# Attention and mixer on one core: two more pairs turned by DMA instead of TensorE, and a turn of u moved from segment 7 to slot 6

## The chip, the cores and the metric

The kernel runs on one core of a Trainium2 chip. The metric is the device time of one execution in microseconds. In the profile's names PE is TensorE (its matmuls), PEld its weight loads, DVE VectorE, ACT ScalarE, POOL GpSimd and SP SyncE, whose queue starts most transfers. The landing of a transfer is the time from its issue to the moment its data are reported as there. A run counts as fast when it is at most 1.5% above the fastest of its kernel.

## The reference

Eight batches of cosine attention with 12 heads, 448 rows and 64 columns per head, followed by a mixer: over the rows ("tok"), then over the columns ("ch").

```python
q_n = q / (norm(q) + 1e-6);  k_n = k / (norm(k) + 1e-6)
x = softmax(q_n @ k_n.T / tau) @ v            # heads side by side: 8 x 448 x 768
u = x + (relu(x.T @ w_tok1) @ w_tok2).T
out = u + relu(u @ w_ch1) @ w_ch2
```

## The kernel before: the parts that matter

Heads go in pairs, six to a batch, 48 in all. Segment i of the main loop computes the scores of pair i, the weighted sum of pair i-1, and pieces ("units") of the last two matmuls of an earlier batch. Two turns (transposes) matter. q and k of a pair must be turned before the scores:

```python
def tpose(i, a0=0, a1=2):                       # TensorE, then DVE copies out of PSUM
    pst = ps.tile([128, a1 - a0, NCH, n], FP16, name=f"pst_{i}_{a0}", tag="b")
    ... eight nc.tensor.transpose ...
    nc.vector.tensor_copy(out=st["qk"][:, a0:a1], in_=pst[:])

def tpose_dma(i):                               # one DMA from SP's queue
    nc.sync.dma_start_transpose(out=st["qk"]..., in_=st["kq16"][:]...)
```

Pairs below `DMA_T0 = 16` use the first, the others the second. And u of each pair must be turned before the "ch" matmuls; for most pairs by DMA, for pairs 2 to 5 on TensorE:

```python
def upose_two(p0, p1):
    psT = ps.tile([128, 2, 4, 128], FP16, name=f"psT_{p0}_{p1}", tag="b")
    ... eight transposes of pairs p0 and p1 ...
    nc.scalar.activation(out=ut[0][:, p0:p1 + 1:p1 - p0], in_=psT[:], func=AF.Copy)
```

The loop (cut):

```python
for i in range(NPAIR + 1, NP_ALL):              # segments 7 to 47
    for c in range(KC): score(i, c)             # psS, wide tiles "s"
    if i == NPAIR + 1:                          # segment 7
        upose(i - 4, 2); tok2(i - 2, pe=True); pv_wide(i - 1)
        upose_two(2, 5); x_wide(i - 1); sums(i + 2)
    else:
        pv_rest(i - 1); pv(i - 1, 0); pv(i - 1, 1)          # psO, small tiles "b"
    ...
    side(i)              # POOL: squares(i+3), scaled(i+2); loads; tpose_dma(i+2)
    unit(True)           # psG or psF
    ...                  # last scores: psS or psQ
    if i > NPAIR + 1: tok2(i - 2)               # psU, then DVE adds x: u
    if i + 1 < DMA_T0: tpose(i + 1)             # pst
    if due(): unit(True)
    tok1(i - 1)                                 # psR, then DVE's max: rt
    sums(i + 3)
```

PSUM has two small tiles ("b": psO, psU, pst, psR) and three wide ones ("s": scores, psG, psF). "Slot 6" is the pass for pair 6, written out ahead of this loop.

## Time and profile before

| | before |
|---|---|
| time, median of the first three runs | 386.81 us (386.41 to 387.72) |
| span of the profiled run | 385.1 us |
| PE (matmul) busy | 97% |
| granted clock | 0.997 |

### The profile page before, as it was taken

To read this page: it belongs to the slowest core of one execution; us is meant where nothing else is said; L and a number is where in the kernel's file an instruction comes from. 1 tells how busy PE (TensorE), PEld (TensorE's weight loads), DVE (VectorE), ACT (ScalarE), POOL (GpSimd) and SP (SyncE) were. 2 spreads that over 40 slices of the span, in tenths; PEclk is the share of its full clock that TensorE was granted. 3 is DMA by queue.
4 is the path that set the end of the run, shared out by engine and by line. 5 is a ranking of instruction groups with operands and counts; after the bars stand their busy time and mean duration, and the time that the engine had idled before them with its cause. 6 is when DMAs were issued, how large, how long until landed. Compare 5 with 4: busy or idle time off the path is not lost.

```text
span 385.1 us, 10228 instructions
## 1 busy us (share of the span) xinstructions
PE 372.8 (97%) x4128; PEld 244.4 (63%) x4128; DVE 217.0 (56%) x517; ACT 227.8 (59%) x399; POOL 238.3 (62%) x383
## 2 busy tenths in 40 slices
PE   5989999999999999999999999999999999999995
PEld 5566666667657666667656666667666666665563
DVE  6789766777536674557545674656544673241041
ACT  5899787746665457855675456854675466601400
POOL 8799997978567577678567667768657733000000
PEclk9999999999999999999999999999999999999998
DMA  8999999993985878868894788968994755013022
GB/s 204 257 239 222 264 243 188 209 215 65 223 191 126 214 184 203 181 156 176 219 190 118 185 192 201 190 173 178 197 217 117 139 124 124 15 56 95 0 77 89
DMA packets 114879, 64.08 MB, mean 166 GB/s; under 512 B 71184, under 2 KB 111248, under 8 KB 114832
## 3 DMA queue, kind: packets, MB, share of 16 engines
q1 hardware_dynamic: 108400, 57.49, 65.8%
q0 software_dynamic: 5616, 5.21, 8.6%
q10 hardware_dynamic: 816, 0.73, 0.7%
q8 instruction: 32, 0.52, 0.6%
q14 instruction: 15, 0.12, 0.1%
HBM read 43.45 MB, written 11.01 MB: 141 GB/s over the span
## 4 chain that ended last, share of the span: by engine, by line
PE 89%; DMA 3%; ACT 2%; DVE 2%; POOL 2%; issue 0%; ACTq 0%; DVEq 0%; POOLq 0%
PE psF L463 28%; PE psG L447 28%; PE psO L362 9%; PE psS L323 8%; PE psU L412 5%; PE psR L398 5%; DMA w2n<-in_moe_w_tok_dram 2%; PE psQ L330 2%; ACT pt L324 1%; PE psO L345 1%; DMA qf<-in_q_dram 1%; DVE ssq L253 1%; POOL kq L276 1%; PE pst L300 1%; PE psO L380 1%; POOL sq L237 1%
## 5 line engine op out<-in xcount | busy, mean ns | idle before, releaser
L324 ACT ACTIVATE pt<-psS 128x896 f16<-128x896 f32 (+1 forms) x156 | 132.6, 916 | 57.7 <-PE psS L323 57.7
L447 PE MATMUL psG<-ut,wc1t 128*128 128x448 f16 x576 | 116.8, 352 | 0.4 <-ACT ut L437 0.4
L463 PE MATMUL psF<-wc2t,gt 128*128 128x384 f16 (+2 forms) x684 | 116.2, 323 | 0.0
L276 POOL TENSOR_TENSOR kq<-kf,rn 128x384 f16<-128x384 f32 (+1 forms) x48 | 42.9, 894 | 73.8 <-DVE rn L262 70.5
L463 PEld LDWEIGHTS <-gt 128*128 128x128 f16 x684 | 64.3, 98 | 38.0
L450 ACT ACTIVATE gt<-psG 128x448 f16<-128x448 f32 x96 | 51.9, 541 | 61.4 <-PE psG L447 61.3
L447 PEld LDWEIGHTS <-wc1t 128*128 128x128 f16 x576 | 53.9, 98 | 44.7 <-issue 0.6
L467 DVE TENSOR_TENSOR ost<-psF,u 128x384 f32<-128x384 f32 (+2 forms) x65 | 34.5, 531 | 57.1 <-PE psF L463 56.9
L253 DVE TENSOR_REDUCE ssq<-sq 128x15 f32<-128x960 f32 (+2 forms) x49 | 55.8, 1141 | 4.7 <-ACT sq L235 3.9
L401 DVE TENSOR_SCALAR rt<-psR 128x256 f16<-128x256 f32 x48 | 20.1, 419 | 59.3 <-PE psR L398 59.2
L276 POOL TENSOR_TENSOR kq<-qf,rn 112x512 f16<-112x512 f32 x45 | 47.0, 1045 | 3.0
L323 PE MATMUL psS<-qk 64*128 64x448 f16 x312 | 41.6, 359 | 2.7 <-DVE qk L302 2.3
L237 POOL TENSOR_TENSOR sq<-qf 112x512 f32<-112x512 f32 x39 | 40.6, 1040 | 0.0
L237 POOL TENSOR_TENSOR sq<-kf 128x384 f32<-128x384 f32 (+1 forms) x46 | 40.2, 873 | 0.0
L362 PE MATMUL psO<-vt,pt 128*128 128x65 f16 (+1 forms) x1024 | 39.1, 193 | 0.0
L362 PEld LDWEIGHTS <-pt 128*128 128x128 f16 (+1 forms) x1024 | 34.2, 97 | 3.6 <-PE psS L323 1.0
L366 DVE TENSOR_TENSOR x<-psO,rec 128x256 f16<-128x256 f32 x82 | 34.8, 425 | 2.8
L415 DVE TENSOR_TENSOR u<-psU,x 128x512 f16<-128x512 f32 x48 | 32.3, 674 | 3.9 <-PE psU L412 2.7
L398 PEld LDWEIGHTS <-w1t 128*128 128x128 f16 x384 | 25.1, 98 | 9.3 <-issue 2.4
L398 PE MATMUL psR<-x,w1t 128*128 128x128 f16 x384 | 29.3, 219 | 0.7 <-DVE u L415 0.7
L412 PEld LDWEIGHTS <-w2t 128*128 128x128 f16 x384 | 24.8, 98 | 7.3 <-issue 1.0
L412 PE MATMUL psU<-rt,w2t 128*128 128x128 f16 x384 | 29.3, 219 | 0.0
(57 smaller groups left out, 289.2 us busy)
## 6 DMA issues: line engine op xcount, KB each, us to landing
qf<-in_q_dram SPq DMA_DIRECT2D x48, 224.0 KB, 4.2
kf<-in_k_dram SPq DMA_DIRECT2D x36, 192.0 KB, 3.6
vf<-in_v_dram SPq DMA_DIRECT2D x36, 192.0 KB, 3.8
vf<-in_v_dram SPq DMA_DIRECT2D x12, 224.0 KB, 7.7
out_dram<-ost SPq DMA_DIRECT2D x8, 336.0 KB, 3.6
wc1t<-in_moe_w_ch_dram POOLq DMA_DIRECT2D x4, 576.0 KB, 9.6
wc2t<-in_moe_w_ch_dram POOLq DMA_DIRECT2D x2, 1152.0 KB, 12.8
out_dram<-ost SPq DMA_DIRECT2D x8, 288.0 KB, 3.6
```

The lines of the kernel that those rows point to most:

```text
L237: nc.gpsimd.tensor_mul(out=dst, in0=src, in1=src)
L253: nc.vector.tensor_reduce(out=st["ssq"][0:n, sl], in_=st["sq"][0:n, sl], axis=AXX.X, op=ALU.add)
L276: eng.tensor_tensor(out=kq[0:p, a, 0:n].rearrange("p c g e -> p g c e"), in0=st["kq"[a]][:].rearrange("p (g c) e -> p g c e", g=2), in1=_b ...
L323: nc.tensor.matmul(psS[:, hh, 0:S], qk[hb, c * n:c * n + 128], qm[hb], start=True, stop=True)
L324: nc.scalar.activation(out=pts[i % 2][0:n, 2 * S * c:2 * S * (c + 1)].rearrange("p (h s) -> p h s", h=2), in_=psS[0:n, :, 0:S], func=AF.Ex ...
L362: nc.tensor.matmul(psO[:, m, 0:E + 1], pts[i % 2][0:n, at:at + 128], vt[0:n, i % HP, nch * hh + c, 0:E + 1], start=(old(i) and c == 0), st ...
L366: nc.vector.tensor_tensor(out=st["x"][:, :, hh * E:(hh + 1) * E], in0=psO[:, :, 0:E], in1=_bcast_free(rec[:], E), op=ALU.mult)
L398: nc.tensor.matmul(psR[:, tt], w1t[:, w1[m], tt * 128:(tt + 1) * 128], st["x"][:, m], start=(m == 0), stop=(m == 3))
L412: nc.tensor.matmul(psU[:, m], w2t[:, tt, lo:lo + 128], st["rt"][:, tt], start=(tt == 0), stop=(tt == TT - 1))
L447: nc.tensor.matmul(psG[:, 0:S], wc1t[:, dt, ct * 128:(ct + 1) * 128], ut[b][:, dt].rearrange("p m s -> p (m s)")[:, lo:lo + S], start=(n = ...
L450: nc.scalar.activation(out=gt[:, ct, (b % 2) * S:(b % 2 + 1) * S], in_=psG[:, 0:S], func=AF.Relu)
L463: nc.tensor.matmul(psF[:, 0:hi - lo], gt[:, ct, at:at + 128], wc2t[:, ct, lo:hi], start=(ct == 0), stop=(ct == CT - 1))
```

## The change

The intent is to take TensorE work away where TensorE is the bound: pairs 14 and 15 are turned by DMA, and u of pair 2 is turned where TensorE waits anyway.

```diff
-    DMA_T0 = 16
+    DMA_T0 = 14
...
-    def upose_two(p0, p1):
-        psT = ps.tile([128, 2, 4, 128], FP16, name=f"psT_{p0}_{p1}", tag="b")
-        for j, pj in enumerate((p0, p1)):
-            for m in range(4):
-                nc.tensor.transpose(psT[:, j, m], u16[0][:, pj, m], id16[:])
-        nc.scalar.activation(out=ut[0][:, p0:p1 + 1:p1 - p0], in_=psT[:], func=AF.Copy)
+    def upose_act(i, wide=False):
+        psT = (ps2 if wide else ps).tile([128, 4, 128], FP16, name=f"psT_{i}", tag="s" if wide else "b")
+        for m in range(4):
+            nc.tensor.transpose(psT[:, m], u16[0][:, i, m], id16[:])
+        nc.scalar.activation(out=ut[0][:, i], in_=psT[:], func=AF.Copy)
...
-        dts = (0, 1, 3, 4, 2, 5) if (b, ct) == (0, 0) else range(DT)
...
         tpose(i + 1)
+        upose_act(i - 4, True)                 # slot 6: pair 2
         norms(i + 2, dve=True)
...
-                upose_two(2, 5)
+                upose_act(i - 2)               # segment 7: pair 5
```

More of the change, by code (lines that the diff above doesn't have):

```diff
@@ L444, in m_ch1 @@
         psG = (ps2 if wide else ps).tile([128, 512], FP32, name=f"psG_{b}_{ct}", tag="s" if wide else "b")
-        dts = (0, 1, 3, 4, 2, 5) if (b, ct) == (0, 0) else range(DT)
-        for n, dt in enumerate(dts):
+        for dt in range(DT):
             nc.tensor.matmul(psG[:, 0:S], wc1t[:, dt, ct * 128:(ct + 1) * 128],
                              ut[b][:, dt].rearrange("p m s -> p (m s)")[:, lo:lo + S],
-                             start=(n == 0), stop=(n == DT - 1))
+                             start=(dt == 0), stop=(dt == DT - 1))
         nc.scalar.activation(out=gt[:, ct, (b % 2) * S:(b % 2 + 1) * S], in_=psG[:, 0:S], func=AF.Relu)
```

## The prediction

> **What bounds the kernel now.** I read the page's first two parts first, to see which engine fills the time and from when.
>
> ```profile
> PE 372.8 (97%) x4128; PEld 244.4 (63%) x4128; DVE 217.0 (56%) x517; ACT 227.8 (59%) x399; POOL 238.3 (62%) x383
> PE   5989999999999999999999999999999999999995
> ACT  5899787746665457855675456854675466601400
> POOL 8799997978567577678567667768657733000000
> PEclk9999999999999999999999999999999999999998
> DMA  8999999993985878868894788968994755013022
> ```
>
> PE (the matmuls) is full from the fourth slice (one slice is 385.1/40 = 9.6 us) to the end, at full clock. The chain that ended last agrees: 89% of it is PE. So after about 38 us, time is gained only where PE work goes, or where PE sits idle. DMA, however, is also nearly full for the first ten slices, just where the change adds transfers. Only the stretch from 38 to 101 us can be touched; after it both kernels issue the same PE work.
>
> I call "segment i" the pass of the loop that computes the scores of pair i; its first scores mark its start in the timeline: segment 7 at 40.49, 8 at 47.66, 12 at 73.03, 13 at 80.25, 14 at 85.96, 15 at 93.04, 16 at 101.15 us. Then I read PE's timeline where the change acts (columns: start, duration, engine, line, operation, tiles, count, idle before).
>
> ```profile
> 39.00 0.56 PE L300 MATMUL pst<-id,kq 112*128 112x112 f16 x8
> 39.95 0.61 PE L398 MATMUL psR<-x,w1t 128*128 128x128 f16 x8 [0.39 <-DVE u L415]
> ...
> 43.09 0.61 PE L436 MATMUL psT<-id,u 128*128 128x128 f16 x8
> 43.53 0.92 PE L447 MATMUL psG<-ut,wc1t 128*128 128x448 f16 x4
> 44.81 0.54 PE L447 MATMUL psG<-ut,wc1t 128*128 128x448 f16 x2 [0.35 <-ACT ut L437]
> ...
> 83.96 0.61 PE L412 MATMUL psU<-rt,w2t 128*128 128x128 f16 x8
> 84.41 0.61 PE L300 MATMUL pst<-id,kq 128*128 128x128 f16 x8
> 85.35 0.61 PE L398 MATMUL psR<-x,w1t 128*128 128x128 f16 x8 [0.33 <-DVE u L415]
> ...
> 90.10 0.61 PE L300 MATMUL pst<-id,kq 128*128 128x128 f16 x8
> 90.55 2.11 PE L463 MATMUL psF<-wc2t,gt 128*128 128x384 f16 x12
> ```
>
> There are three PE waits here: 0.39 us in slot 6 and 0.33 us in segment 13, both for an addition on DVE that frees a small score-bank ("b") tile, and 0.35 us in segment 7 for ACT's copy of the turned u. The starts show the real cost of eight transposes: 90.55 - 90.10 = 0.45 us, 56 ns each, not the 0.61 us that a pipelined group's duration suggests.
>
> **What the Trainium skill says.** "TensorE: Matmul & The Clock Gate", section "Wait — 56ns, not 53.3ns?", puts matmuls of 128 columns 55.6 ns apart at full clock; the trace agrees (56 ns). "VectorE: DVE Perf Modes", section "The three transpose paths", gives 1309 ns for one 128x128 turn by the DMA crossbar. Here eight of them in one transfer land 3.2 us after issue at the median over 32 transfers, so the trace shows the batch to be far cheaper than eight times that. "DMA: Bandwidth & Descriptors", section "Queues, rings and completion order", says that each DMA engine takes turns between the queues that have work, and takes one queue's descriptors in order. The trace agrees: the transposes of u that were issued while the second weight load of wc2t (1152 KB, another queue, issued at 69.80) was under way landed after 8.7 us (issued at 71.82) and 6.0 us (at 78.24), the one at 85.33 after 2.8 us. This matters below.
>
> **The change, part by part.**
>
> *Segment 13: tpose(14) leaves PE.* The eight transposes at 84.41 go. The transposes also took a "b" tile; with only two of those in turn, tok1's psR then had to take the tile of psU, and waited for DVE to add u out of it. Without pst, psR takes the other one, which x released at about 82.95. Nothing else stands between, so psR starts at 84.41 instead of 85.35: gain 0.94 us (0.45 work, 0.49 wait by the starts).
>
> *Segment 14: tpose(15) leaves PE.* psF follows without a wait on either side, so the gain is 90.55 - 90.10 = 0.45 us. The two copies out of PSUM on DVE (0.68 us each) go as well, beside other work: worth nothing directly.
>
> *Slot 6: four transposes of u of pair 2 move in.* They need 4 x 0.056 = 0.22 us. They stand after pst (ends in starts at about 39.40) and before psR at 39.95, which waits for DVE anyway. Their tile is a wide score tile, last read by x at 38.38 to 39.07, so it is free. Cost 0. ACT's copy of 512 columns I estimate at 0.6 us, from 1.02 us for 1024 and 0.54 us for 448. It runs from about 40.2 to 40.8, in a hole of ACT (it waited 0.64 us until 40.89 for scores). psS(7,2), which takes the same wide tile next, is wanted at 40.94: just free.
>
> *Segment 7: only pair 5 is turned.* Four transposes instead of eight; they wait slightly for u of pair 5 (DVE 42.42 + 0.68 = 43.10), so they start at about 43.16 and the first psG matmul at about 43.39 instead of 43.53. ACT's copy starts at about 43.58, ends near 44.18; psG's sixth matmul, the only one to need it, comes up after five at 0.19 us, at 44.34. So the ACT wait disappears. The last two matmuls, which began at 44.81, begin at 44.15: 0.66 us earlier on PE.
>
> But not all of that survives. In this segment ACT is pinned by DVE: the Ln starts at 45.38 behind the sum of squares, which follows x, which nothing here moves. Its order is then
>
> ```profile
> 45.72 0.22 ACT L265 ACTIVATE ne<-rn 112x16 f32<-112x16 f32 x1
> 45.84 0.53 ACT L450 ACTIVATE gt<-psG 128x448 f16<-128x448 f32 x1
> 46.26 0.91 ACT L324 ACTIVATE pt<-psS 112x896 f16<-112x896 f32 x1
> 47.31 0.54 ACT L450 ACTIVATE gt<-psG 128x448 f16<-128x448 f32 x1
> ```
>
> With PE earlier, the second Relu can start at about 47.10, right behind the exponential, and no sooner. It frees the wide tile that psS(8,2) takes next (three in turn). So psS(8,2) comes at about 47.70; before it came at 47.66 + 0.45 = 48.11. I count 0.41 us of the 0.66.
>
> Sum: 0.94 + 0.45 + 0 + 0.41 = 1.80 us. 386.81 - 1.80 = 385.0 us.
>
> **The rivals.** *First: the new DMA transposes come late, and the scores wait for them.* POOL finishes scaling two pairs ahead 6.9 us into a segment (79.92 in segment 12, 87.14 in 13). Segment 12 lasts 7.22 us, the shortened 13 5.71 - 0.94 = 4.77 us. So qk of pair 14 has 7.22 + 4.77 - 6.9 = 5.1 us from issue to use, that of pair 15 has 4.77 + 7.08 - 0.45 - 6.9 = 4.5 us. The quiet landing is 3.1 to 3.2 us, which fits both. Against: 5.0 to 8.7 us under the weight load would not fit. For: the wc2t burst is nearly drained when pair 14's transpose is issued, its packets thin out at 80 to 81 us; the loads of the same segment are now behind the transpose, not ahead of it; and the DMA engines have almost nothing to do from 86 to 93 us, so pair 15 is safe. If pair 14 came as late as 6 to 8 us, that would be 1 to 3 us of PE wait: 386 to 388 us. I give it about one in eight.
>
> *Second: POOL becomes the bound.* Its work in a segment adds up to 5.2 to 5.5 us, more than the new 4.77 us of segment 13.
>
> ```profile
> 84.28 0.83 POOL L276 TENSOR_TENSOR kq<-kf,rn 128x384 f16<-128x384 f32 x1 [1.83 <-DVE rn L262]
> ...
> 89.98 0.83 POOL L276 TENSOR_TENSOR kq<-kf,rn 128x384 f16<-128x384 f32 x1 [0.30 <-DVE rn L262]
> ...
> 97.06 0.83 POOL L276 TENSOR_TENSOR kq<-kf,rn 128x384 f16<-128x384 f32 x1 [1.65 <-DVE rn L262]
> ```
>
> It would lag about 0.6 us in segment 14, but what it makes is needed two segments later, and segment 15 gives it 1.65 us to catch up. Time unchanged, 385.0.
>
> *Third: the gain of segment 7 goes wholly or not at all.* If the ring of wide tiles does not bind, all 0.66 us stay: 384.8. If the copy in slot 6 delays psS(7,2) and with it the exponentials, nothing stays: 385.4.
>
> *Fourth: later loads are late,* since on SP's queue those of pairs 18 and 19 now stand behind transposes that wait for POOL until 79 and 86 us. They are squared three segments ahead of use, from segment 15 (91 us) on, and landings are 3 to 5 us. Unchanged.
>
> **Range and chances.** The three runs before span 386.41 to 387.72, so a median moves by some 0.4 us by itself. The low end takes 0.66 in segment 7 and a lucky median: 384.2. The high end takes one late transpose of about 1 us or a gain of segment 7 lost: 386.2. The change touches about 2 us of 387, 0.5%; 2% would be 7.7 us, which neither the gain nor the worst late landing reaches. Faster by over 2%: 0.01; within 2%: 0.98; slower: 0.01.
>
> **What would show each step.** Right: after psU of segment 13 psR follows at once, without the wait on DVE; segment 13 lasts about 4.8 us and segment 14 about 6.6; no ACT wait before the last psG matmuls of segment 7; segment 7 to 8 is about 0.4 us shorter by the third score of segment 8; the two new qk transposes land within 3 to 4.5 us and no scores of pairs 14 or 15 wait for DMA; from 101 us on the same lengths as before. Wrong: a PE idle before the scores of pair 14 that the DMA ended; a landing above 5 us; segments 8 to 11 of another length than before; or a copy of u on ACT much longer than 0.6 us.

## More of the kernel before

The prediction shows the lines of the page and reads them. I add one line, from the list of waits of the kernel before in the window 84 to 87 us (who waited, for whom: us in total, times, longest). I had not used it:

```profile
PEld L323 <- DVE qk L302: 0.2, 1, 0.2
```

In segment 13 the weight load for the scores of pair 14 also waited a little for DVE's copy of the turned pair, behind the two waits that I did see.

## The result, and the profile after

| | before | after |
|---|---|---|
| first measurement, median of four runs each | 386.97 us | 384.38 us (384.1 to 385.77) |
| ratio, 95% interval | | 0.9939 (0.991 to 0.9969) |
| second measurement, 11 and 5 runs | 386.34 | 384.46 (383.85 to 384.81), ratio 0.9946 |
| third measurement, 11 and 6 runs | 386.58 | 384.79 (384.5 to 385.95), ratio 0.9955 |

A ratio is the mean time of one kernel's fast runs over that of the other's in the same rounds, so not quite the ratio of the medians. By the medians the gain is 2.59, 1.88 and 1.79 us in the three measurements. The prediction said 385.0 (384.2 to 386.2) and a gain of 1.80 us.

The traces tell it more sharply than the times. The start of the kernel varies from run to run with the landing of the w2n weights (the "tok2" weights). These are lines of the chain that ended last, first of before, then of after (start, us, what):

```profile
10.54 8.27 DMA w2n<-in_moe_w_tok_dram
```

```profile
10.87 8.85 DMA w2n<-in_moe_w_tok_dram
```

Here the weights of after landed 0.91 us later (19.72 against 18.81), and segment 7 began at 41.41 instead of 40.49 us. In two further traces of the same kernel after, it began at 39.73 and 40.35 us, and in the trace of another kernel below at 39.37. So about 2 us between single runs come from the start, where the two kernels issue the same work but for the four transposes and the copy in slot 6. These move nothing there: from the landing of w2n to segment 7 it was 21.67 us in before and 21.69 in after. In 8 of the 14 traces it was 21.65 to 21.69 us; in the other six it was 22.0 to 22.6 us, so there the landing alone did not set it. From the start of segment 7 to that of segment 16, however, the three traces of after give 58.97, 58.98 and 58.98 us. Before gave 60.66 in its one trace; its segments come back to within 0.01 us wherever an experiment below leaves them alone. The change is worth 1.69 us in this stretch. After it the two kernels keep step: the lead of after grows by only 0.02 us from segment 16 to the last full segment.

By segment, from the starts of the first scores:

| segment | 7 | 8 | 12 | 13 | 14 | 15 |
|---|---|---|---|---|---|---|
| before | 7.17 | 6.90 | 7.22 | 5.71 | 7.08 | 8.11 |
| after | 6.52 | 7.17 | 7.23 | 4.70 | 6.78 | 8.10 |

Lines of the page of after (busy time by engine; busy tenths in 40 slices):

```profile
PE 371.8 (97%) x4112; PEld 243.3 (63%) x4112; DVE 216.0 (56%) x515; ACT 227.8 (59%) x400; POOL 238.3 (62%) x383
PE   5889999999999999999999999999999999999995
```

PE has 16 matmuls fewer and is as full as it was. The lines of PE's timeline that answer to those of the prediction (start, us, engine, line, operation, tiles, count, idle before):

```profile
40.32 0.39 PE L435 MATMUL psT<-id,u 128*128 128x128 f16 x4
40.87 0.61 PE L398 MATMUL psR<-x,w1t 128*128 128x128 f16 x8 [0.16 <-DVE u L415]
...
44.09 0.40 PE L435 MATMUL psT<-id,u 128*128 128x128 f16 x4
44.32 1.30 PE L445 MATMUL psG<-ut,wc1t 128*128 128x448 f16 x6
...
47.93 1.02 PE L323 MATMUL psS<-qk 64*128 64x448 f16 x6
...
84.51 0.61 PE L412 MATMUL psU<-rt,w2t 128*128 128x128 f16 x8
84.96 0.61 PE L398 MATMUL psR<-x,w1t 128*128 128x128 f16 x8
85.50 0.74 PE L323 MATMUL psS<-qk 64*128 64x448 f16 x6
86.08 0.43 PE L345 MATMUL psO<-vt,pt 64*128 64x65 f16 x8
```

The reader should see five things. In slot 6 the four transposes fill the wait: psR waits 0.16 instead of 0.39 us. In segment 7 psG runs in one piece of six. In segment 13 psR follows psU after 0.45 us, without a wait. But the six scores of segment 8 take 1.02 us instead of 0.74, so 0.28 us of the gain of segment 7 is given back. And the first psO of segment 14 takes 0.43 us instead of 0.28, a new wait of 0.15 us.

ACT in segments 7 and 8 of after (timeline, columns as above) shows why the scores wait:

```profile
44.52 0.60 ACT L436 ACTIVATE ut<-psT 128x512 f16<-128x512 f16 x1 [0.17 <-PE psT L435]
46.30 0.31 ACT L264 ACTIVATE rn<-ssq,tiny 112x16 f32<-112x16 f32 x1 [1.19 <-DVE ssq L253]
...
47.99 0.55 ACT L448 ACTIVATE gt<-psG 128x448 f16<-128x448 f32 x1
```

The copy took the 0.60 us I had estimated. ACT then stood 1.19 us waiting for DVE's sum of squares, and the second Relu, which frees the wide tile for the third scores of segment 8, ended at 48.54. The traced landings of the two new transposes, from issue, were 4.9 us for pair 14 and 3.1 us for pair 15. Pair 14 was issued at 80.53 us and its first scores came at 85.50, so it had under 0.1 us to spare.

The second rival, POOL, also shows, and as small as foretold (timeline of after):

```profile
90.18 0.83 POOL L276 TENSOR_TENSOR kq<-kf,rn 128x384 f16<-128x384 f32 x1
...
96.30 0.83 POOL L276 TENSOR_TENSOR kq<-kf,rn 128x384 f16<-128x384 f32 x1 [0.68 <-DVE rn L262]
```

In segment 14 POOL no longer waits; in segment 15 it has caught up.

### The profile page after: what moved, and what is told of

The parts are those of the page before. It is cut to its first block, busy times and chain, and to the rows that moved or that the text cites. A ratio compares the mean times of both kernels' runs of the same rounds, so it can differ in the third digit from the quotient of the medians.

```text
span 384.0 us, 10193 instructions
## 1 busy us (share of the span) xinstructions
PE 371.8 (97%) x4112; PEld 243.3 (63%) x4112; DVE 216.0 (56%) x515; ACT 227.8 (59%) x400; POOL 238.3 (62%) x383
## 4 chain that ended last, share of the span: by engine, by line
PE 88%; DMA 3%; ACT 3%; DVE 2%; POOL 2%; issue 1%; ACTq 0%; DVEq 0%; POOLq 0%
PE psF L461 28%; PE psG L445 28%; PE psO L362 9%; PE psS L323 8%; PE psU L412 5%; PE psR L398 5%; DMA w2n<-in_moe_w_tok_dram 2%; PE psQ L330 2%; ACT pt L324 1%; PE psO L345 1%; DVE ssq L253 1%; DMA qf<-in_q_dram 1%; POOL kq L276 1%; PE pst L300 1%; PE psO L380 1%
```

## The experiments

My theory: the gain is the sum of three local shares in segments 7, 13 and 14, and the surplus of the first measurement is startup and scatter. The rivals: a further real gain that my sum misses; that the segment 13 share is only TensorE work; and that the DMA turns are hidden anyway, so that more of them would be better still. Twelve experiments ran, nine new kernels and three repeats. All gave correct results.

**Only the DMA part.** The kernel before with one line changed:

```diff
-    DMA_T0 = 16
+    DMA_T0 = 14
```

> The kernel before, with only the limit moved: pairs 14 and 15 turned by DMA, the turning of u as before. My theory (the shares add up): from the start of segment 7 to the start of segment 16 this trace is 1.3 us shorter than before (60.66 us before, so 59.3 to 59.4), 1.0 us of it in segment 13 and 0.3 us in segment 14; segment 7 is unchanged at 7.17 us. The median time is 1.3 us below before, give or take 0.5 for the weight load that starts the pipeline early or late. Rival (the measured 2.4 to 2.6 us is a real gain that my sum of 1.8 misses, and it sits in the DMA part): over 1.8 us below before.

Measured: median 384.85 us against 386.34, ratio 0.9959 (0.9945 to 0.9972). Segment 7 was 7.17 us, unchanged; from segment 7 to 16 it took 59.42 us, 1.24 us less than before. So the sum held (1.49 us by the medians, 1.24 by the trace). The split did not: segment 13 took 4.92 us and segment 14 6.63, where after has 4.70 and 6.78. The reason is in this run's timeline of PE and its landing:

```profile
85.52 0.74 PE L323 MATMUL psS<-qk 64*128 64x448 f16 x6 [0.15 <-DMA qk<-kq]
```

```profile
DMA to landing us min/median/max: 5.1/5.1/5.1
```

Here the transpose of pair 14 landed after 5.1 us and the scores waited for it. The wait of psO in segment 14 did not show behind that one. The first rival of my prediction is real, and only just held off in after.

**Only the turn of u.** The kernel after with the limit put back:

```diff
-    DMA_T0 = 14
+    DMA_T0 = 16
```

> The kernel after with the limit put back: pairs 14 and 15 on TensorE, u of pair 2 turned in slot 6 and that of pair 5 alone. My theory: from the start of the first scores of segment 7 to those of segment 9 this trace is 0.37 us shorter than before (14.07 us before, so about 13.7), segments 13 and 14 are unchanged at 5.71 and 7.08 us, and the third scores of segment 8 wait about 0.3 us for ACT as in the trace of after. Median time 0.4 us below before, within the scatter. Rival (the startup of the kernel after is itself shorter because four transposes moved into it): segment 7 starts earlier than the 40.49 us of before in this run and in after, and the gain is 0.8 us or more.

Measured: segments 7 and 8 took 6.53 + 7.16 = 13.69 us, segments 13 and 14 were 5.70 and 7.08, all as my theory had it; 0.39 us less from segment 7 to 16. Its median was 386.18 against 386.34 us, ratio 0.9996 (0.9983 to 1.0009), so the time alone could not tell 0.4 us. Segment 7 began at 39.42 us in this trace, which by itself would speak for the rival; but the kernel after, with the same startup, had begun it at 41.41. The startup does not distinguish the kernels: w2n landed at 17.25 us here and at 19.72 in after.

**Only pair 15 by DMA.** The kernel after with `DMA_T0 = 15`:

```diff
-    DMA_T0 = 14
+    DMA_T0 = 15
```

> The kernel after with only pair 15 turned by DMA, pair 14 on TensorE. My theory: segment 13 is back at 5.71 us (psR waits for DVE again), segment 14 is 0.45 us shorter than the 7.08 us of before (6.63), as psO of segment 14 no longer waits; from segment 7 to 16 in all 0.37 + 0.45 = 0.82 us shorter than before. Median 0.8 us below before. Rival (the two DMA turns are worth the same each, half of what both give): segment 14 shorter by about 0.65 us.

Measured: segment 13 5.70 us with the wait for DVE back (0.34 us), segment 14 6.63 us, 59.82 us from segment 7 to 16, 0.84 less than before; median 385.7 (0.64 us below before, where 0.8 was expected), ratio 0.9974. The trace is as expected: pair 15 is worth its 0.45 us of work. Pair 14 is worth 1.00 us in segment 13 and costs 0.15 us in segment 14.

**The kernel after again.** No edit.

> The kernel after, unchanged, once more with five rounds, to learn how far from 1.7 us (what its trace shows from segment 7 on) the gain in time lies. My theory: the surplus of the first measurement was startup and scatter, so the gain over before comes out between 1.3 and 2.2 us, and the start of segment 7 in this trace differs from the 41.41 us of the first one with the landing of the w2n weights. Rival: a further real gain of 0.7 us that the first trace hid; then the gain is again 2.4 us or more in all rounds.

Measured: 384.46 against 386.34 us, 1.88 us by the medians, 58.98 us from segment 7 to 16; segment 7 at 39.73. The surplus of 0.7 us was not repeated.

**Pair 13 by DMA too.** The kernel after with the limit one lower:

```diff
-    DMA_T0 = 14
+    DMA_T0 = 13
```

> The kernel after with pair 13 turned by DMA too (the limit one lower). Its transpose is issued in segment 11 at about 74.5 us, in the middle of the second weight load of wc2t, and is needed at the start of segment 13, about 5.9 us later. Theory of the late landing (the first rival of the prediction): turns of u issued in that load landed after 6 to 9 us, so this one lands after 6 to 9 us and the scores of pair 13 wait 0.5 to 3 us for it; the 0.45 us of TensorE work saved in segment 12 is eaten, and segments 12 and 13 together are longer than in after (11.93 us). Theory that a transfer of qk is hidden anyway: it lands within 5.5 us, segment 12 is 0.45 us or more shorter, and the time is 0.5 us below after.

Measured: the profiled run took 390.95 us, the median was 387.22 (385.89 to 390.95) against 386.87 for before, ratio 1.0008 (0.9982 to 1.0035). All of the gain is lost, and the profiled run is the slowest of the six, so its waits are not typical of them. The times scatter over 5.06 us, against 0.41 us for the best kernel below. In the trace segment 12 took 10.82 us and 13 6.23, together 17.05 instead of 11.93. Timeline of PE, the landing of pair 13, and the traffic of the DMA queues in the window 74 to 78 us (packets, MB, share of the engines):

```profile
83.79 0.76 PE L323 MATMUL psS<-qk 64*128 64x448 f16 x6 [3.97 <-DMA qk<-kq]
```

```profile
DMA to landing us min/median/max: 9.6/9.6/9.6
```

```profile
q0 software_dynamic: 996, 0.76, 132.5%
q1 hardware_dynamic: 6, 0.00, 0.3%
```

The transpose was issued at 74.13 us. For four microseconds the weight load (q0) moved 996 packets and SP's queue (q1) six. It landed even later than I expected, and the wait of 3.97 us was longer. A second loss came behind it, in the stretches of PE's timeline after the wait (PE, PEld, DVE, ACT and POOL busy with counts, then granted clock, DMA share, GB/s):

```profile
83.79:86.02 2.23, 2.23 (x38) 1.86 (x39) 0.40 (x2) 1.82 (x3) 0.00 (x0) 0.63 1.21 283
86.02:88.84 2.82, 2.82 (x16) 1.48 (x14) 1.25 (x5) 1.12 (x3) 0.97 (x2) 0.68 1.13 147
```

After the idle time the clock was 0.63 and 0.68 of full speed in these two stretches, 5.05 us together. In finer stretches it was 1.00 up to 84.20 us, 0.50 from 84.70 to 87.70 and 1.00 again from 88.20, in all about 3.4 us at half. Segment 13 was 1.53 us longer than in after. The Trainium skill, "TensorE: Matmul & The Clock Gate", section "What's actually happening", says that an idle window of about 3.4 us halves TensorE's clock until it has again been busy for such a window. This trace agrees, with 3.97 us of idle time and about 3.4 us at half clock. Being late by 4 us cost 5.1 us.

**DVE's sum first.** One line of the kernel after moved:

```diff
                 pv_wide(i - 1)
+                sums(i + 2)
                 upose_act(i - 2)
                 x_wide(i - 1)
-                sums(i + 2)
```

> The kernel after with one line moved: in segment 7 DVE sums the squares of pair 9 before it makes x of pair 6. My theory: in after the third scores of segment 8 wait 0.28 us for the second Relu, which ACT reaches late because Ln waits 1.2 us for that sum. Here Ln starts about 1 us earlier after its copy of u, the six scores of segment 8 take 0.74 us again instead of 1.02, and the stretch from segment 7 to 9 is 0.28 us shorter than in after (13.69, so about 13.4). Rival (the wide tile is late for another reason, or x of pair 6 being later costs as much): no change or longer.

Measured: segments 7 and 8 took 6.52 + 6.90 us, 0.27 us less than after, and 58.71 us from segment 7 to 16. Timeline of ACT, then of PE:

```profile
43.53 0.60 ACT L436 ACTIVATE ut<-psT 128x512 f16<-128x512 f16 x1 [0.17 <-PE psT L435]
44.20 0.31 ACT L264 ACTIVATE rn<-ssq,tiny 112x16 f32<-112x16 f32 x1
```

```profile
46.94 0.74 PE L323 MATMUL psS<-qk 64*128 64x448 f16 x6
```

Ln follows the copy at once, and the scores of segment 8 take 0.74 us again. So the 0.28 us that segment 8 gave back was indeed the wide tile held by a Relu that a sum on DVE had pushed back. Median 384.36 us against 386.87, ratio 0.9941 (0.9922 to 0.9959).

**The work back without the tile.** The kernel after, with a dummy in segment 13 before tok1:

```diff
             if i + 1 < DMA_T0:
                 tpose(i + 1)
+            if i == 13:
+                warm(8, True)
```

> The kernel after with eight dummy matmuls of 128 columns into a wide tile where the turn of pair 14 stood in segment 13: TensorE's work is back, the small score-bank tile and the DVE copy are not. My theory: of the 1.01 us won in segment 13 the work is 0.45, so segment 13 is 4.70 + 0.45 = 5.15 us, and psR does not wait for DVE; segment 14 may win back the 0.14 us that psO waits in after. Rival (all of the gain in segment 13 was work, or the wait returns with any work there): 5.7 us.

Measured: segment 13 5.15 us, segment 14 6.63. Both as expected: eight matmuls cost 0.45 us, and the wait of psO goes. PE's timeline, with no wait before psR:

```profile
83.75 0.61 PE L314 MATMUL warm<-id 128*128 128x128 f16 x8
84.19 0.61 PE L398 MATMUL psR<-x,w1t 128*128 128x128 f16 x8
```

**The tile back, first try.** The same with `warm(1)`, one matmul into a small tile:

```diff
+            if i == 13:
+                warm(1)
```

> The kernel after with one dummy matmul into a small score-bank tile where the turn of pair 14 stood: the tile is taken again, the work (0.05 us) is not. My theory: psR again takes the tile of psU and waits for DVE's addition; psR starts about 1.0 us after psU ends its issue less the copy, so segment 13 is about 4.70 + 0.9 = 5.6 us, against 5.71 before. Rival (the tile is not what held psR): 4.75 us.

Measured: segment 13 4.97 us, nearer to the rival's number. But the experiment was badly built. Nothing reads the dummy's tile, so the tile framework gave that very tile to psR: in the trace psR's first matmul waits for a semaphore that only PE raises, and not for DVE. psR began 0.27 us after the dummy started, where 0.06 would be its issue; the dummy itself lasted 0.22 us, so psR waited for its result. The run tells nothing about psU's tile.

**The tile back, held.** The same, with a reader on DVE:

```diff
+            if i == 13:
+                w = ps.tile([128, 128], FP32, name="held", tag="b")
+                nc.tensor.matmul(w[:], id16[:], id16[:], start=True, stop=True)
+                got = att.tile([128, 4], FP32, name="got", tag="rec")
+                nc.vector.tensor_copy(out=got[:], in_=w[:, 0:4])
```

> The run with the dummy matmul again, built rightly: this time DVE reads four columns of the dummy's small tile, so that the tile is held until after DVE's addition, as the copy of the turned pair held it before, and psR has to take the tile of psU. The work put back is one matmul (0.06 us). My theory (the tile, not the work, was over half of the gain in segment 13): psR waits for DVE's addition and starts about 1.35 us after psU instead of 0.45, so segment 13 is 4.70 + 0.9 = 5.6 us. Rival (the tile did not matter): about 4.8 us.

Measured, PE's timeline:

```profile
84.45 0.61 PE L412 MATMUL psU<-rt,w2t 128*128 128x128 f16 x8
84.90 0.22 PE L694 MATMUL held<-id 128*128 128x128 f16 x1
85.84 0.61 PE L398 MATMUL psR<-x,w1t 128*128 128x128 f16 x8 [0.72 <-DVE u L415]
```

psR starts 1.39 us after psU, exactly as before the change, with one dummy matmul instead of eight transposes; segment 13 is 5.64 us against 5.71. So with the tile held, the eight transposes cost almost nothing: they lie inside the wait for DVE. With the tile free, they cost 0.45 us. Taking away the work alone gains at most 0.07 us (5.71 - 5.64; DVE's copy of the turned pair is gone here too), the tile and that copy alone 0.56 (5.71 - 5.15, the run before the last), and both gained 1.01. With the copy gone in both runs, the tile alone is worth 0.49 (5.64 - 5.15), though the second of them has eight dummy matmuls and the first only one.

**A unit moved to segment 13.** The kernel with the sum first, and:

```diff
-            if due():
+            if due() or i == 13:
                 unit(True)
```

> The kernel with DVE's sum moved forward, and one unit of the last matmuls (1.95 us) moved from segment 14 to segment 13, between psU and psR. My theory: pair 14 then has 6.9 us from issue to use instead of 5.0, so no late landing can reach the scores, and psO of segment 14 has no wait; but the same wait of 0.14 us comes up in segment 15 instead, since segment 14 now has no unit between psU and psR. Segments 13, 14 and 15: 6.65, 4.7 and 8.24 us; sum of segments 7 to 15 the same 58.7 us as with the sum alone. Rival (the wait belongs to the short segment 13 alone): 58.57 us.

Measured: segments 13, 14 and 15 took 6.65, 4.70 and 8.23 us, and 58.70 from segment 7 to 16, as expected. The wait of psO moved on to segment 15 with the short segment, so in both runs it came behind the segment without a unit between psU and psR. Pair 14 landed after 4.9 us, with 2 us to spare now. The five times were 383.91 to 384.32 us, median 384.31, against 384.79 (384.5 to 385.95) for after on the same chip, with no overlap; ratio to before 0.9936 (0.9924 to 0.9947). In this one measurement this version beats both kernels. Its median is no better than that of the sum alone (384.4, next); it differs by its scatter.

**The sum first, again.** No edit against the earlier run.

> The kernel with DVE's sum moved forward, once more, on the same chip as the kernel after: by the traces it is 0.27 us (0.07%) faster than after, which five rounds will hardly resolve; the median is expected 0 to 0.5 us below that of after, its trace from segment 7 to 16 58.7 us.

Measured: median 384.4 us, as expected, but 383.74 to 387.51, and the run of 387.51 was the profiled one. It caught the late landing in the act (PE's timeline; pair 14 landed after 6.3 us):

```profile
87.41 0.74 PE L323 MATMUL psS<-qk 64*128 64x448 f16 x6 [1.33 <-DMA qk<-kq]
```

The same kernel, with a transpose that landed after 6.3 instead of 4.7 us: the scores of pair 14 waited 1.33 us and segment 13 took 6.10 us. The second loss of this run, about 1.1 us in segment 7, is a stall before the second score of pair 7 which the profile gives once to an ACT result and once to PE's own issue; I leave its cause open. Why the DMA queues ran late in this run I can only describe: POOL waited twice for a late load of k, and SP's loads of segments 6 to 11 came some microseconds later than in the third trace of after. In the 5 us after the issue of pair 14 the weight load's queue still moved 344 packets; in the second trace of after it moved 3.

**After, a third time.** No edit.

> The kernel after a third time, beside the two others: 58.97 us from segment 7 to 16 as in both earlier traces, and a median 1.5 to 2.4 us below before. If its landing of pair 14 goes over 5.0 us in this trace, the scores of pair 14 wait as they did in the run that moves only the limit.

Measured: 384.79 against 386.58 us, 1.79 by the medians, 58.98 us from segment 7 to 16, landing 4.9 us and no wait for DMA.

## Why the prediction was right

**The sum.** Predicted 1.80 us; 1.69 by the trace, 1.79 to 2.59 by medians. The number and the mechanism hold; three terms of the sum were a little off: segment 13 by +0.07, segment 14 by -0.15, segment 7 by -0.03 us. They partly cancel: the terms are off by 0.25 us in all, the sum by 0.11, and that much is luck. So is the first median, near the low end of the range; it was not repeated.

**Segment 13, "gain 0.94 us (0.45 work, 0.49 wait by the starts)".** It was 1.01. The missing 0.07 is DVE's copy of the turned pair, which the scores of pair 14 waited for behind psR; I had said that the copies are "worth nothing directly". The experiments showed besides that work and wait are not two separate gains: the work lay inside the wait.

**Segment 14, "the gain is 90.55 - 90.10 = 0.45 us".** Right for pair 15 alone. In the full change 0.15 us is given back at psO, because rt, DVE's reading of psR, now ends only just before psO wants that tile: DVE made it from 85.76 to 86.17 us, behind its addition of u, and the weight loads of psO went on at 86.23. The profile names no releaser for this wait; the times do. With "Nothing else stands between" I had looked for the next instruction's wait in segment 13 and not for the next user of each small tile.

**Slot 6, "Cost 0".** Right: the wait for DVE shrank from 0.39 to 0.16 us around the four transposes.

**Segment 7, "I count 0.41 us of the 0.66".** It was 0.65 on PE and 0.38 after the wide tile. (The list of signs of being wrong names segments 8 to 11 "of another length than before". Segment 8 is, 7.17 against 6.90 us, but by the very wait that this step foretold; the sign was badly put. Segments 9 to 11 are unchanged.) Moving the sum forward brought the other 0.27 back, which shows the step.

**The rivals.** The late landing was the right one to fear, and its room was nearly right (5.1 us foretold, 4.97 in after). What failed is the expected landing, "within 3 to 4.5 us": pair 14 took 4.7 to 5.1 us in nine traces, 6.0 in the run with pair 13 and 6.3 in one. That its scores did not wait in after was luck, by under 0.1 us. My argument that the weight load "is nearly drained" was true in most runs, but the weight load is not what makes the 4.9 us. In the 5 us after the issue its queue moved 3 packets in the second trace of after and 4 in the run with the moved unit, and pair 14 landed after 4.9 us all the same. It moved 251 in the run with only the DMA part (5.1 us) and 344 in the run of 6.3 us, so a load under way seems to add to it, though 144 in the first run with the sum moved went with 4.7 us. The trace of before, which I had, shows such landings elsewhere (its 32 transposes of qk):

```profile
DMA to landing us min/median/max: 3.1/3.2/5.9
```

Taken one by one, 7 of these 32 landed after more than 4.5 us, all issued after 100 us, when no weight load was running. I had set the room against the median and not against this spread. Why about one landing in five takes so long stays open. POOL lagged in segment 14 and caught up, as said. The later loads cost nothing in the traces of after.

**What stays open.** Where the surplus of the first measurement came from is not settled. The startup varies by 2 us in single traces, and the stretch from the start of the last full segment to the end by 0.7 (56.94 to 57.64 us over all traces; 57.31 in before, 57.03 in after), so both leave room for scatter; no trace shows a further gain by the change. How often the kernel after meets a landing over 5 us is not known either; one of its 15 runs took 385.95 us and another 385.77, and the profiled one of these two had a late start and no DMA wait.

## What to carry to other kernels

Before counting the work that a change removes from the bound engine, ask whether that work lies inside a wait; here freeing a tile was worth about half a microsecond by itself (0.49 to 0.56), and removing the work at most 0.07. When a turn moves to DMA, compare its room with the longest landings of its kind and not with the median: about 5.0 us of room against a median of 3.2 us looked safe, just held at 4.9, and broke at 5.1 (by 0.15 us) and at 6.3. If the order of independent work can widen the room at no cost, as the moved unit did, do it; in its one measurement of five runs the times also scattered less (0.41 us, against 1.45 for after).

## What the Trainium skill lacked or had wrong

- "VectorE: DVE Perf Modes", section "The three transpose paths", gives 1309 ns for one 128x128 turn by DMA and no landing time for several in one transfer. Here eight in one transfer landed after 3.2 us at the median and 3.1 us at best, after more than 4.5 us in 7 of the 32 transfers of before with no weight load running, and after 9.6 us in the middle of a weight load.
- "DMA: Bandwidth & Descriptors", section "Queues, rings and completion order", says that each engine takes turns between the queues that have work. In the run with pair 13, while a transpose stood issued on SP's queue, the weight load's queue moved 996 packets in 4 us and SP's queue 6. In the next 2 us they moved 360 and 306, which looks like taking turns. The section does not lead one to expect that an issued transpose can show no packets for so long first; which part of the path held it was not found. The landings that the prediction gives as agreeing (8.7 and 6.0 us) show the delay, not the turns.
- "Perfetto Trace Analysis", section "Optimization Strategy", advises to look for the gaps on the bound engine. It does not say that removed work may lie inside such a gap: eight transposes cost 0.45 us with the tile free and at most 0.07 us with it held.
- No page that I used says what a matmul into a small tile costs when the next matmul takes the same tile: psR began 0.27 us after the start of a single dummy matmul, where matmuls without such a wait follow after 0.06 us.
- "TensorE: Matmul & The Clock Gate" was right in both places used: 56 ns a matmul of 128 columns, and a halved clock (0.50 for about 3.4 us) after an idle time of 3.97 us.
